# Grouped attention and a spectral filter on one core: queries kept in DRAM, longer batches, and the filter's last part turned

## The chip, the core and the metric

The kernel runs on one core of a Trainium2 chip. Times are microseconds of the device (us) for one execution. The core has five engines that this document speaks of: PE (matrix multiplications, with PEld as its loads of stationary operands), ACT (ScalarE, here above all `exp`), DVE (VectorE), POOL (GpSimd) and SP, which here only issues DMAs. Matrix products are written to PSUM, eight banks of 128 x 512 float32; everything else is in SBUF or in DRAM.

## The reference

The two halves of the output have nothing to do with each other. The first is attention of 16 query heads over one common head of keys and values, the second a filter in the frequency domain:

```python
B, S, D, H = 1, 2048, 448, 16; Dh = 28
# first half
q = (A_x @ wq) per head;  k = A_x @ wk;  v = A_x @ wv
p = softmax(q @ k.T * Dh**-0.5);  a = concat_heads(p @ v) @ wo
# second half
X = rfft2(B_x) * (w_r + 1j*w_i);  b = irfft2(X)      # 2048 x 448
out = concatenate([a, b], axis=-1)
```

All inputs and outputs are float32.

## The kernel before

**Stages.** The first 70 us project the queries, keys and values and run the first part of the filter. From there on the program is one long weave: attention, in which PE, ACT and DVE hand tiles to each other, with pieces of the filter and of the output projection pushed in between. A short tail finishes the last 512 rows of the first output.

**Attention.** The 2048 queries are 4 chunks `c` of 512; the 16 heads are 4 groups `g` of 4; the 2048 keys are 16 blocks `kc` of 128. A *step* is one (c, g, kc): four score matmuls, one per head, each 128 keys x 512 queries into a PSUM bank (line 872); four tiles of `exp` on ACT (line 816) into two buffers of 2 x 512 columns; and the products with the values (line 827), four heads side by side in 32 columns of the array, summed over the 16 `kc` in one PSUM bank `po`. In the trace a float32 product shows as two instructions, so the value products of a step are 8 rows of line 827. There are 256 steps. Scores and value matrices use different precisions: operands of type float32r (`qa`, `ka`) run in one pass; where float32 exactness is wanted the kernel splits an operand in a high part and a rest and adds three such products (`mm3`).

**Batches.** Steps are handled in batches. A batch first issues all its score matmuls and then, in `flush`, the value products of its steps (without its last one, but with the last one of the batch before, `kept`). So PE goes from scores to value products and back once per batch. The scores of the last step of a batch come early among the others (token `k`): DVE copies them from PSUM into the buffers `k` (line 878), and ACT makes their `exp` in place as two instructions of 128 x 1024 (line 895) while PE is busy with the value products. That keeps ACT fed while no new scores come.

**The table of order.** PE, ACT and DVE run in the order in which the Python code records their instructions. `PLAN` has one string per batch, made by `spread(n, units, ...)`: `-` is a score matmul whose `exp` ACT makes from PSUM, `k` one that DVE copies away, `e` one of the last step that ACT reads from PSUM itself. Letters are *units*: `A` and `B` are the second part of the filter (`fft2_a`, `fft2_b`), `W` is one of four pieces of an output projection of 128 rows (`wo_unit`), `Z` a piece of the filter's third part. In front of all this, `take()` hands out the PSUM bank that by the planner's clocks comes free first, `put()` queues DVE work that may be done later, and `passed()` and `at_once()` move the clocks and record queued work when its time has come.

**The third part of the filter** works on 8 slices `q`. `fft3_a` (line 660, twice per slice, e = 0 and 1) makes the spectrum over rows in float32, and DVE copies it to `z` (line 663). `fft3_b` (line 674, twice per slice, v = 0 and 1) multiplies with the cosines and sines `cs3`: the spectrum is the stationary operand, the constants are the 113 moving columns, in float32; its result has rows of the image on the 128 partitions. DVE makes a sum and a difference from PSUM (lines 678 to 680), POOL two further sums (lines 684 and 685), and SP writes 128 x 452 to `ob`.

**Queries.** `qraw` holds all projected queries in SBUF (128 x 4 x 2048). For each group `build_q` takes one chunk of it, shifts it, splits it on DVE into `qh` and `ql`, and SP places these by nine DMAs in `qa`, of which there are two. After its chunk's four groups are built, a chunk of `qraw` is read only in a branch for very large scores, which the inputs do not take.

**Tail.** The last group's values are divided and transposed on DVE; `partial` adds up three of four groups for each of four blocks of rows, `final` adds the fourth with float32 operands (line 918); ACT copies the block from PSUM (line 741) and issues its DMA.

Of the kernel before, what the change touches and what calls it, by code (L numbers as in the profile page):

```python
# [37 lines left out]
def spread(n, units, lazy=4, start=0.9, rest=0.85):  # L38

    m = 4 * n - 4  # L40
    out = [(float(i), "-") for i in range(m)]
    out += [(j + 0.5 if j < lazy else m + 0.1 * j, "k" if j < lazy else "e") for j in range(4)]
# [4 lines left out]
PLAN = ["eeee"] + ["eeeeF"] + [spread(2, "", 0, 1.05)] + 3 * [spread(2, "", 0)] + [spread(5, "A", 4, 1.6)]  # L47
PLAN += [spread(5, "BA", 4, 0.9, 0.6)] + [spread(5, "A")] + 6 * [spread(5, "BA", 4, 0.9, 0.6)]
PLAN += [spread(5, "BA", 4, 0.75, 0.6)] + 3 * [spread(5, "BA", 4, 0.9, 0.6)] + 2 * [spread(6, "X")]
PLAN += [spread(5, "BA", 4, 0.9, 0.6)] + [spread(6, "BAX")] + [spread(5, "BAB", 4, 0.9, 0.6)]  # L50
PLAN += [spread(6, "BX")] + [spread(6, "Y")] + [spread(5, "")] + 2 * [spread(6, "Y")]
PLAN += [spread(6, "Y", 4, 0.9, 0.6)] + [spread(6, "X")] + [spread(6, "X", 4, 0.9, 0.6)] + [spread(6, "X")]
PLAN += [spread(6, "Y")] + [spread(6, "X", 4, 0.9, 0.6)] + 3 * [spread(6, "Y")]
PLAN += [spread(6, "Y", 4, 0.9, 0.73)] + [spread(6, "Y")] + [spread(6, "Y", 4, 0.9, 0.73)]
PLAN += 3 * [spread(6, "X")] + [spread(6, "Y")] + [spread(6, "X", 4, 0.9, 0.73)] + [spread(5, "Y")]
PLAN += [spread(6, "Y")] + [spread(6, "Y", 4, 1.2)] + [spread(5, "Y")]
# [6 lines left out]
def kernel(ctx: ExitStack, tc: tile.TileContext, t: dict):  # L63
# [17 lines left out]
    bits = cp.tile([1, 1], F32, name="bits")  # L81
    t1 = dp.tile([128, 32, DF], F32, name="t1")
# [428 lines left out]
    pp = pools.enter_context(tc.tile_pool(name="pp", bufs=P_BUFS))  # L511
# [125 lines left out]
    def fft3_consts():  # L637
        fc["cs3"] = fp.tile([113, 4, 113], F32, name="cs3", tag="cs", bufs=1)
        behind(nc.gpsimd.dma_start(fc["cs3"], t["cs3"]), begun[-1])
# [15 lines left out]
    def fft3_a(q, e):  # L655
# [6 lines left out]
        z = c2["z", q, e] = fp.tile([113, 2, 4, 64], F32, name=f"z{e}", tag=("wi", "cst")[e])  # L662
        nc.vector.tensor_copy(z[:w], pz[:w].rearrange("p j (r n) -> p r j n", r=2))
        at_once()
        give(bank)

    def fft3_b(q, v):
        ze, zo = c2["z", q, 0], c2["z", q, 1]
        cs3 = fc["cs3"]
        js = slice(2 * v, 2 * v + 2)  # L670
        bank = take()
        py = bank[:, :452].rearrange("p (k n) -> p k n", k=4)
        for k, (z, w, r) in enumerate(((ze, 113, 0), (zo, 112, 0), (zo, 112, 1), (ze, 113, 1))):
            mm(py[:, k], z[:w, r, js], cs3[:w, k], start=True, stop=True)  # L674
        passed(888)
        y1 = fp.tile([128, 2, 2, 113], F32, name="y1", tag="pwr")
        m = fp.tile([128, 2, 113], F32, name="m", tag="us", bufs=1)
        nc.vector.tensor_copy(m, py[:, 2:4])
        nc.vector.tensor_tensor(y1[:, :, 0], py[:, 0:2], m, op=ALU.add)
        nc.vector.tensor_tensor(y1[:, :, 1], py[:, 0:2], m, op=ALU.subtract)  # L680
        at_once(1100)
        give(bank)
        yo = fp.tile([128, 4, 113], F32, name="yo", tag="pwi")
        nc.gpsimd.tensor_tensor(yo[:, 0:2], y1[:, 0], y1[:, 1], op=ALU.add)  # L684
        nc.gpsimd.tensor_tensor(yo[:, 2:4], y1[:, 0], y1[:, 1], op=ALU.subtract)
# [242 lines left out]
    for k in (0, 1):  # L928
        partial(k)
# [197 lines left out]
```

## Time and profile before

| | before |
|---|---|
| median of 3 runs | 642.26 us (642.26 to 642.81) |
| the profiled execution | 642.82 us, its span 641.0 us |
| PE busy | 635.7 us, 99% |
| ACT busy | 550.7 us, 86% |
| DVE busy | 372.3 us, 58% |
| POOL busy | 80.1 us, 12% |
| granted TensorE clock | 1.00 |

PE is busy nearly all the time by this count, but the count has the overlap of successive matmuls and any short wait inside a row in it. Where PE loses time has to be read from the starts of its instructions in the timeline: the distance from one start to the next, against what the same kind of instruction takes elsewhere.

### The profile page before, as it was taken

What the parts mean: (1) busy time and instruction counts of PE and PEld (TensorE: products, weight loads), DVE (VectorE), ACT (ScalarE), POOL (GpSimd) and SP (SyncE); (2) the same over time, 40 slices, a digit from 0 to 9 for tenths busy, and PEclk for the clock granted to TensorE, in tenths of its full rate; (3) what the DMA queues carried; (4) which work ended last, traced back from release to release, by engine and by line L of the source; (5) the groups of instructions that cost most, each with busy time, mean ns of one, the idle gap of its engine ahead of it and who ended that gap; (6) DMA issues with size and microseconds to landing.
All of it is one profiled execution on the core that took longest, in us unless ns stands there. A gap on an engine that the chain in (4) does not pass through costs nothing.

```text
span 641.0 us, 12024 instructions
## 1 busy us (share of the span) xinstructions
PE 635.7 (99%) x4470; PEld 381.8 (60%) x4470; DVE 372.3 (58%) x683; ACT 550.7 (86%) x1011; POOL 80.1 (12%) x150
## 2 busy tenths in 40 slices
PE   9999999999999999999999999999999999999997
PEld 6877655556555556655655566556655566556555
DVE  5999628889997934766543523264545332264521
ACT  5554999999999998988899898998999898998981
POOL 3021401011311110000120300003031100200110
PEclk9999999999999999999999999999999999999999
DMA  8755971554835521214241403123241303140001
GB/s 271 268 161 159 262 175 47 143 126 111 205 102 128 142 59 49 79 47 136 63 103 44 115 16 85 39 57 92 55 120 43 88 15 81 44 127 2 30 31 60
DMA packets 36113, 63.83 MB, mean 100 GB/s; under 512 B 7905, under 2 KB 23922, under 8 KB 35084
## 3 DMA queue, kind: packets, MB, share of 16 engines
q1 hardware_dynamic: 30832, 49.60, 28.0%
q0 software_dynamic: 4640, 12.48, 7.8%
q10 hardware_dynamic: 576, 0.92, 0.4%
q8 instruction: 36, 0.59, 0.4%
q14 instruction: 29, 0.24, 0.1%
HBM read 30.04 MB, written 14.75 MB: 70 GB/s over the span
## 4 chain that ended last, share of the span: by engine, by line
PE 98%; DMA 1%; ACT 0%; SPq 0%; issue 0%; ACTq 0%
PE s L872 31%; PE s L827 22%; PE sx L827 9%; PE s L347 6%; PE po L872 5%; PE po L827 4%; PE s L736 4%; PE sx L872 4%; PE s L145 2%; PE s L674 2%; PE s L660 2%; PE pbb L164 1%; DMA raw<-wq 1%; PE s L562 1%; PE s L561 1%; PE s L563 1%
## 5 line engine op out<-in xcount | busy, mean ns | idle before, releaser
L816 ACT ACTIVATE p<-s 128x512 f32<-128x512 f32 x650 | 345.9, 631 | 33.4 <-PE s L872 27.5
L872 PE MATMUL s<-qa,ka 128*128 128x512 f32 x798 | 236.1, 405 | 0.0
L872 PEld LDWEIGHTS s<-qa,ka 128*128 128x128 f32 x798 | 146.7, 188 | 67.7 <-issue 26.8
L878 DVE COPY k<-s 128x512 f32<-128x512 f32 x129 | 82.5, 682 | 106.6 <-PE s L872 106.6
L827 PE MATMUL s<-p,vs 128*32 128x512 f32 x1024 | 121.7, 595 | 0.0
L895 ACT ACTIVATE k<-k 128x1024 f32<-128x1024 f32 x88 | 90.3, 1108 | 0.0
L827 PEld LDWEIGHTS s<-p,vs 128*32 128x32 f32 x1024 | 30.8, 109 | 67.6 <-issue 65.6
L816 ACT ACTIVATE p<-po 128x512 f32<-128x512 f32 x89 | 56.2, 631 | 9.2 <-PE po L872 8.5
L816 ACT ACTIVATE p<-sx 128x512 f32<-128x512 f32 x85 | 53.6, 630 | 3.1 <-PE sx L872 1.9
L827 PE MATMUL sx<-p,vs 128*32 128x512 f32 x416 | 49.3, 594 | 0.0
L872 PE MATMUL po<-qa,ka 128*128 128x512 f32 x120 | 49.2, 410 | 0.0
L872 PE MATMUL sx<-qa,ka 128*128 128x512 f32 x106 | 42.4, 400 | 0.0
L700 POOL DMA_DIRECT2D ol<-ol x36 | 18.1, 510 | 135.9 <-DVE ol L723 69.0
L827 PE MATMUL s<-k,vs 128*32 128x512 f32 x256 | 33.4, 594 | 0.0
L684 POOL TENSOR_TENSOR yo<-y 128x226 f32<-128x226 f32 x16 | 9.5, 596 | 188.0 <-DVE y L680 110.9
L872 PEld LDWEIGHTS po<-qa,ka 128*128 128x128 f32 x120 | 22.5, 188 | 14.6 <-issue 9.2
L827 PEld LDWEIGHTS sx<-p,vs 128*32 128x32 f32 x416 | 12.5, 110 | 27.9 <-issue 27.6
L831 DVE STREAM_TRANSPOSE osb<-s 128x512 f32<-128x512 f32 x10 | 7.2, 715 | 37.0 <-PE s L827 37.0
L878 DVE COPY k<-po 128x512 f32<-128x512 f32 x29 | 19.8, 681 | 14.3 <-PE po L872 14.3
L827 PE MATMUL po<-p,vs 128*32 128x512 f32 x208 | 25.0, 595 | 0.0
L872 PEld LDWEIGHTS sx<-qa,ka 128*128 128x128 f32 x106 | 19.9, 188 | 6.7 <-issue 2.5
L347 PE MATMUL s<-xh,wqh 128*128 128x512 f32 x56 | 23.0, 410 | 0.1
(217 smaller groups left out, 788.1 us busy)
## 6 DMA issues: line engine op xcount, KB each, us to landing
qa<-qa SPq DMA_DIRECT2D x15, 512.0 KB
raw<-xa SPq DMA_DIRECT2D x16, 256.0 KB
xb<-xb SPq DMA_DIRECT2D x8, 512.0 KB
qa<-qh SPq DMA_DIRECT2D x64, 64.0 KB
qa<-ql SPq DMA_DIRECT2D x60, 64.0 KB
ob<-yo SPq DMA_DIRECT2D x16, 226.0 KB
t<-bs SPq DMA_DIRECT2D x16, 225.0 KB
wr<-wr POOLq DMA_DIRECT2D x16, 225.0 KB, 4.2
```

The lines of the kernel that those rows point to most:

```text
L145: mm(pa[r0:r0 + 32, e, o0:o0 + n], f[:, 2 * r + k, 2 * p + e, h], cs1[:, 2 * r + k, :n], start=True, stop=True)
L347: mm(pq, w[:, j, gs], x[:, j], start=(j == 0 and n == 0), stop=(j == 3 and n == 1))
L660: mm(pz[:w, j], c2["c", q][:, j, o0:o0 + w], c2["F", q][:, j], start=True, stop=True)
L674: mm(py[:, k], z[:w, r, js], cs3[:w, k], start=True, stop=True)
L684: nc.gpsimd.tensor_tensor(yo[:, 0:2], y1[:, 0], y1[:, 1], op=ALU.add)
L700: nc.gpsimd.dma_start(ol[c][o, g].bitcast(F32), ol[c][r, 0].bitcast(F32))
L736: mm(p, x[c][:, g, s], w, start=(g == 0 and n == 0), stop=(g == NG - 1 and n == 2))
L816: nc.scalar.activation(tiles[-1][:, h % 2], sc, AF.Exp, scale=SCALE)
L827: mm(po[c, g][32 * i:32 * i + 32], vs[:, kc], ps[i // 2][:, i % 2], start=(n == 1), stop=(n == 16))
L872: begun.append(mm(sc, ka[:, kc * 128:(kc + 1) * 128], qa[c, g][:, h], start=True, stop=True))
L878: nc.vector.tensor_copy(keep[h // 2][:, h % 2], sc)
L895: nc.scalar.activation(p, p, AF.Exp, scale=SCALE)
```

## The change

The edit has five parts.

1. **Queries in DRAM.** When the last group of a chunk has been built, SP copies the chunk of `qraw` to a new DRAM tile `qd` (three times, 1 MB each), and its place in SBUF becomes two more buffers for `exp` tiles. The eight buffers `p` are now named tiles that pass through a queue `spans`. Only the branch for large scores reads `qd` back.
2. **Longer batches.** `PLAN` is written anew. From step 102 on a batch has 6, 7 or 8 steps; there are 46 batches instead of 50 (2 of one step, 4 of two, 1 of four, 14 of five, 5 of six, 18 of seven, 2 of eight; before 2, 4, 0, 18, 26, 0, 0). In 24 batches with more than four `k` or `e`, the last *two* steps are put aside: the second-last one in two buffers of `spans`, with its value products at the end of the same flush, the last one in `k` as before. Copies `k` are spread over more of the batch.
3. **The filter's third part.** `fft3_a` splits its result in a high part and a rest on DVE. `fft3_b` is turned: the constants, split once, are the stationary operand, and the spectrum is 256 moving columns, in three float32r products for each of two terms. The result has 113 columns of the image on the partitions. The last sum and difference are now made on DVE, once per slice, instead of on POOL, and go out as 112 partitions and one single row (`oc`).
4. **Tail.** `final` uses three float32r products instead of a float32 one, for which DVE splits the last values; the DMAs of the first three blocks are issued by SP, and the last block is copied half by ACT and half by DVE.
5. **Order.** `build_q` for the next group is recorded two steps earlier.

```diff
-def spread(n, units, lazy=4, start=0.9, rest=0.85):
+def spread(n, units, lazy=4, start=0.9, rest=0.85, apart=1.0):
+    late = 8 if lazy > 4 else 4
+    m = 4 * n - late
...
-PLAN += [spread(6, "Y")] + [spread(6, "Y", 4, 1.2)] + [spread(5, "Y")]
+PLAN += [spread(7, "ZZ", 8, 0.9, 0.6, 2.0)] + [spread(7, "ZZ", 8, 0.6, 0.85, 2.0)]
...
-    pp = pools.enter_context(tc.tile_pool(name="pp", bufs=P_BUFS))
+    pp = pools.enter_context(tc.tile_pool(name="pp", bufs=1))
+    spans = deque(pp.tile([128, 2, CW], F32, name=f"p{i}") for i in range(P_BUFS))
...
-        z = c2["z", q, e] = fp.tile([113, 2, 4, 64], F32, name=f"z{e}", tag=("wi", "cst")[e])
-        nc.vector.tensor_copy(z[:w], pz[:w].rearrange("p j (r n) -> p r j n", r=2))
-        at_once()
+        ...
+        z = pz[:w].rearrange("p j (r n) -> p r j n", r=2)
+        nc.vector.tensor_copy(h[:w], z)
+        nc.vector.tensor_tensor(l[:w], z, h[:w].bitcast(F32), op=ALU.subtract)
+        at_once(1330)
...
-        for k, (z, w, r) in enumerate(((ze, 113, 0), (zo, 112, 0), (zo, 112, 1), (ze, 113, 1))):
-            mm(py[:, k], z[:w, r, js], cs3[:w, k], start=True, stop=True)
+        py = bank[:113].rearrange("p (k n) -> p k n", k=2)
+        for i, k in enumerate((v, v + 2)):
+            ...
+            a, b = fc["cs3h"][:w, k], fc["cs3l"][:w, k]
+            mm(py[:, i], a, h, start=True, stop=False)
+            mm(py[:, i], b, h, start=False, stop=False)
+            mm(py[:, i], a, l, start=False, stop=True)
...
-        nc.gpsimd.tensor_tensor(yo[:, 0:2], y1[:, 0], y1[:, 1], op=ALU.add)
-        nc.gpsimd.tensor_tensor(yo[:, 2:4], y1[:, 0], y1[:, 1], op=ALU.subtract)
-        r0 = (2 * q + v) * 128
-        nc.sync.dma_start(t["ob"][r0:r0 + 128], yo)
+        if v:
+            x0, d = c2["y", 0], fp.tile([113, 2, 256], F32, name="yo", tag="pwi")
+            def total():
+                nc.vector.tensor_tensor(x, x0, x, op=ALU.add)
+                nc.sync.dma_start(t["ob"][q, 0], x[:112])
+                nc.sync.dma_start(t["oc"][q:q + 1], x[112:113])
+            def difference():
+                nc.vector.tensor_tensor(d, x0, x, op=ALU.subtract)
+                nc.sync.dma_start(t["ob"][q, 1], d[:112])
+            put(("y", q), [(600, difference), (600, total)], True)
...
+        c, g = divmod(step, 64)
+        if c < NC - 1 and g == 40:
+            need(("q", 4 * c + 3))
+            behind(nc.sync.dma_start(qd[:, :, c * CW:(c + 1) * CW], qraw[:, :, c * CW:(c + 1) * CW]), begun[-1])
+        if c < NC - 1 and g == 43:
+            spans.extend(qraw[:, i:i + 2, c * CW:(c + 1) * CW] for i in (0, 2))
-        if step % 16 == 3 and step < 240:
+        if step % 16 == 1 and step < 240:
...
+        stay = 1 + (sum(k in "ke" for k in tokens) > 4)
+        keep = [[pp.tile([128, 2, CW], F32, name="k", bufs=4) for _ in range(2)]]
+        if stay > 1:
+            keep.append([spans.popleft() for _ in range(2)])
...
-        flush(steps[:1] + kept if n > 4 else kept + steps[:-1], steps[1:-1] if n > 4 else [])
-        kept = steps[-1:]
+        flush(normal[:1] + kept if n > 4 else kept + normal, normal[1:] if n > 4 else [])
+        kept = [(*s, ps, False) for s, ps in zip(steps[:-stay - 1:-1], keep)]
+        for i in reversed(range(stay)):
+            ...                                   # exp of keep[i]
+            if i:
+                flush([kept.pop()])
+                spans.extend(keep[i])
...
     def final(k):
-        p = ws[k]
-        mm(p, on[:, 128 * k:128 * k + 128], w3, start=False, stop=True)
-        wo_out(p, c, k, True)
+        p, s = ws[k], slice(128 * k, 128 * k + 128)
+        h, l = oh[c][:, NG - 1, s], ol[c][:, NG - 1, s]
+        mm(p, h, woh[:, NG - 1], start=False, stop=False)
+        mm(p, l, wox[:, NG - 2], start=False, stop=False)
+        mm(p, h, wol[:, NG - 1], start=False, stop=True)
+        wo_out(p, c, k, k + 1)
```

What this does to the order of instructions is seen at three places. The first is `fft3_b` on PE, the first of it, in the kernel before (names carry the tile's number behind the last underscore; `s0` to `s5`, `sx` and `po` are PSUM banks; line 872 are scores, line 674 is `fft3_b`, `z0` and `z1` the spectrum for e = 0 and 1):

```order
L872 MATMUL po_1105<-qa_3142,ka_67 128x512
L674 MATMUL s3_87<-cs3_1346,z0_3392 128x113
L674 MATMUL s3_87<-cs3_1346,z1_3398 128x113 x2
L674 MATMUL s3_87<-cs3_1346,z0_3392 128x113
L674 MATMUL s4_88<-cs3_1346,z0_3392 128x113
L674 MATMUL s4_88<-cs3_1346,z1_3398 128x113 x2
L674 MATMUL s4_88<-cs3_1346,z0_3392 128x113
L872 MATMUL s2_86<-qa_3142,ka_67 128x512
```

And the first `fft3_b` of the changed kernel on PE (line 917 are scores now, lines 699 to 701 the three products; `zh` and the reused tile `c2` are the high parts, `zl` the rests):

```order
L917 MATMUL sx_1113<-qa_2972,ka_67 128x512
L699 MATMUL s2_87<-zh_3228,cs3h_3122 113x256
L700 MATMUL s2_87<-zh_3228,cs3l_3123 113x256
L701 MATMUL s2_87<-zl_3229,cs3h_3122 113x256
L699 MATMUL s2_87<-c2_3124,cs3h_3122 113x256
L700 MATMUL s2_87<-c2_3124,cs3l_3123 113x256
L701 MATMUL s2_87<-zl_3258,cs3h_3122 113x256
L917 MATMUL s1_86<-qa_2972,ka_67 128x512
```

Four products of 113 columns have become six of 256 columns, and the second unit, which followed at once (bank `s4`), now stands apart among the scores.

The second place is the end of a flush on PE, in a batch of six steps before (line 827 are the value products, summed in the bank `po_1105`; a row stands for two heads of a step):

```order
L827 MATMUL po_1105<-k_3105,vs_68 32x512 x2
L827 MATMUL po_1105<-k_3106,vs_68 32x512 x2
L827 MATMUL po_1105<-p_3236,vs_68 32x512 x2
L827 MATMUL po_1105<-p_3246,vs_68 32x512 x2
L827 MATMUL po_1105<-p_3251,vs_68 32x512 x2
L827 MATMUL po_1105<-p_3256,vs_68 32x512 x2
L827 MATMUL po_1105<-p_3268,vs_68 32x512 x2
L827 MATMUL po_1105<-p_3287,vs_68 32x512 x2
L827 MATMUL po_1105<-p_3305,vs_68 32x512 x2
L827 MATMUL po_1105<-p_3308,vs_68 32x512 x2
L872 MATMUL s4_88<-qa_2830,ka_67 128x512
```

And the end of a flush of a batch of seven in the changed kernel on PE (line 863 are the value products; `p0` to `p7` are the named buffers, `qraw` the buffers in the place of the queries, four heads of a step in one row):

```order
L863 MATMUL s4_89<-k_3205,vs_68 32x512 x2
L863 MATMUL s4_89<-p6_1057,vs_68 32x512 x2
L863 MATMUL s4_89<-p7_1058,vs_68 32x512 x2
L863 MATMUL s4_89<-p4_1055,vs_68 32x512 x2
L863 MATMUL s4_89<-p5_1056,vs_68 32x512 x2
L863 MATMUL s4_89<-qraw_66,vs_68 32x512 x4
L863 MATMUL s4_89<-p0_1051,vs_68 32x512 x2
L863 MATMUL s4_89<-p1_1052,vs_68 32x512 x2
L863 MATMUL s4_89<-p2_1053,vs_68 32x512 x2
L863 MATMUL s4_89<-p3_1054,vs_68 32x512 x2
L917 MATMUL s2_87<-qa_2972,ka_67 128x512
```

The flush has seven steps instead of six between two turns to scores, and its last two rows read the two buffers (`p2`, `p3`) of the second-last step, which was put aside.

The third place is ACT around a flush before, where the two instructions of the last step (line 895) stand between the `exp` tiles (line 816) of two batches:

```order
L816 ACTIVATE p_3423<-s4_88 128x512
L816 ACTIVATE p_3423<-sx_1104 128x512
L816 ACTIVATE p_3426<-s5_89 128x512
L816 ACTIVATE p_3426<-s3_87 128x512
L895 ACTIVATE k_3353<-k_3353 128x1024
L895 ACTIVATE k_3354<-k_3354 128x1024
L816 ACTIVATE p_3459<-s1_85 128x512
L816 ACTIVATE p_3459<-s4_88 128x512
L816 ACTIVATE p_3469<-s5_89 128x512
L816 ACTIVATE p_3469<-po_1105 128x512
```

And ACT around a flush of a batch of seven in the changed kernel (line 852 for tiles from PSUM, lines 928 to 946 for the steps put aside: `p2` and `p3` the second-last, `k` the last):

```order
L852 ACTIVATE p1_1052<-s0_85 128x512
L852 ACTIVATE p1_1052<-s1_86 128x512
L928 ACTIVATE p3_1054<-sx_1113 128x512
L928 ACTIVATE p3_1054<-s5_90 128x512
L946 ACTIVATE p2_1053<-p2_1053 128x512 x2
L942 ACTIVATE k_3333<-k_3333 128x1024
L942 ACTIVATE k_3334<-k_3334 128x1024
L852 ACTIVATE p6_1057<-s2_87 128x512
L852 ACTIVATE p6_1057<-s3_88 128x512
L852 ACTIVATE p7_1058<-s0_85 128x512
L852 ACTIVATE p7_1058<-sx_1113 128x512
L852 ACTIVATE p4_1055<-s2_87 128x512
```

ACT now has two steps put aside between the tiles of two batches instead of one, and the first of them (`p3` from PSUM, `p2` in place) feeds the end of the flush that is already running.

More of the change, by code (lines that the diff above doesn't have):

```diff
@@ L33 @@
 P_BUFS = 8
-def spread(n, units, lazy=4, start=0.9, rest=0.85):
-    m = 4 * n - 4
+def spread(n, units, lazy=4, start=0.9, rest=0.85, apart=1.0):
+    late = 8 if lazy > 4 else 4
+    m = 4 * n - late
     out = [(float(i), "-") for i in range(m)]
-    out += [(j + 0.5 if j < lazy else m + 0.1 * j, "k" if j < lazy else "e") for j in range(4)]
+    out += [(apart * j + 0.5 if j < lazy else m + 0.1 * j, "k" if j < lazy else "e") for j in range(late)]
     out += [(m * (j + start) / (len(units) + rest) - 0.4, u) for j, u in enumerate(units)]
@@ L805 @@
     kept, po = [], {}
[L807 removed]
+    waiting, count = deque(), {}
     def exps():
[L811 removed]
+        while waiting and (waiting[0][2] % 2 or spans):
             sc, tiles, h = waiting.popleft()
             if h % 2 == 0:
[L814 to L815 removed]
+                tiles.append(spans.popleft())
             nc.scalar.activation(tiles[-1][:, h % 2], sc, AF.Exp, scale=SCALE)
@@ L836, in flush @@
             if normal:
-                held[0] -= 2
+                spans.extend(ps)
                 exps()
@@ L858 @@
         new, lazy, x = [], [], {"-": 0, "k": 0}
-        keep = [pp.tile([128, 2, CW], F32, name="k", bufs=4) for _ in range(2)]
+        stay = 1 + (sum(k in "ke" for k in tokens) > 4)
+        keep = [[pp.tile([128, 2, CW], F32, name="k", bufs=4) for _ in range(2)]]
+        if stay > 1:
+            keep.append([spans.popleft() for _ in range(2)])
         for k in tokens:
```

139 lines of the change are left out of this document (81 added, 58 removed).

## The prediction

> **What bounds the kernel now.** I read the page first: who is busy, and which engine carries the chain that ended last.
>
> ```profile
> span 641.0 us, 12024 instructions
> PE 635.7 (99%) x4470; PEld 381.8 (60%) x4470; DVE 372.3 (58%) x683; ACT 550.7 (86%) x1011; POOL 80.1 (12%) x150
> PE 98%; DMA 1%; ACT 0%; SPq 0%; issue 0%; ACTq 0%
> ```
>
> PE is on 98% of the chain. So an edit is worth what it takes off PE's row of work, or off the waits in that row. The other engines matter where they make PE wait. The timeline of PE shows one batch of six steps, from flush to flush:
>
> ```profile
> 335.12 1.06 PE L827 MATMUL s<-p,vs 128*32 128x512 f32 x8
> ...
> 340.40 0.50 PE L872 MATMUL sx<-qa,ka 128*128 128x512 f32 x1
> ...
> 340.98 1.33 PE L872 MATMUL s<-qa,ka 128*128 128x512 f32 x5
> 342.14 0.40 PE L872 MATMUL sx<-qa,ka 128*128 128x512 f32 x1
> ...
> 343.77 1.04 PE L660 MATMUL po<-fi,c 128*113 128x128 f32 x8
> ...
> 345.44 1.17 PE L872 MATMUL s<-qa,ka 128*128 128x512 f32 x4
> ```
>
> Durations overlap, so I go by starts. A score takes 0.233 us (340.98 to 342.14 for five). A value product takes 0.1075 us: the next view, the chain in order of time, has runs of 40 in 4.43 and of 48 in 5.29, so 0.86 per step and 0.13 that each run adds. The first two scores after a flush take 0.58 (340.40 to 340.98), 0.11 more than two others. The last score before a flush takes 0.34, again 0.11 more (106.41 to 106.75, second fence below). So a turn to the value products and back costs 0.13 + 0.11 + 0.11 = 0.35 us per batch.
>
> ```profile
> 70.52 2.16 PE s L872 x8
> 96.31 4.43 PE s L827 x40
> 230.81 2.22 PE s L736 x11
> 335.19 5.29 PE s L827 x48
> 626.45 3.85 PE s L736 x18
> ```
>
> ```profile
> 105.10 0.37 PE L561 MATMUL s<-bh,g1h 128*128 128x450 f32 x1
> ...
> 105.71 0.40 PE L872 MATMUL sx<-qa,ka 128*128 128x512 f32 x1
> ...
> 106.41 0.42 PE L872 MATMUL s<-qa,ka 128*128 128x512 f32 x1
> 106.75 1.06 PE L827 MATMUL s<-p,vs 128*32 128x512 f32 x8
> ...
> 356.88 1.04 PE L674 MATMUL po<-cs,z 113*128 113x113 f32 x8
> ...
> 358.59 1.40 PE L872 MATMUL s<-qa,ka 128*128 128x512 f32 x5
> ```
>
> Here are the units: two `fft3_b` in 1.71 us (356.88 to 358.59), 0.855 each, and three float32r products of 450 columns in 0.61 (105.10 to 105.71), 0.203 each. Two `fft3_a` take 1.67 (343.77 to 345.44), and the eleven products of four `W` 2.22.
>
> With these, a batch has a floor: steps x (4 x 0.233 + 0.86) + 0.35 + its units. Stages between two flushes' ends show how far the real ones lie above it (first column the stage in us, then its length, PE, PEld, DVE and ACT busy):
>
> ```profile
> 142.74:153.26 10.52, 10.52 (x70) 6.00 (x66) 9.78 (x19) 9.83 (x18) 0.53 (x1) 1.00 0.34 100
> 317.45:327.47 10.02, 10.02 (x64) 4.64 (x61) 5.84 (x11) 9.42 (x18) 2.54 (x5) 1.00 0.25 59
> 458.62:471.78 13.16, 13.16 (x93) 7.49 (x89) 8.02 (x16) 11.98 (x22) 5.08 (x9) 1.00 0.47 117
> 471.78:484.62 12.84, 12.84 (x92) 7.60 (x88) 3.86 (x6) 11.89 (x22) 0.00 (x0) 1.00 0.22 63
> 563.93:577.24 13.31, 13.31 (x88) 7.92 (x84) 9.30 (x18) 12.00 (x22) 0.00 (x0) 1.00 0.43 114
> ```
>
> The first, five steps with an `A` and a `B`, has a floor of 10.53: no stall, although DVE is 93% busy. The second has no unit: floor 9.31, stall 0.7; ACT is what it waits for, with 9.4 us of work. The third (two `fft3_b`, and DVE with query and output work as well) stalls 0.3, the fourth 0.05, the fifth (one `W` block) 0. Over all 256 steps the floor is 239 (1024 scores) + 220 (2048 value rows) + 20 (`A`, `B`) + 27 (`W`) + 27 (`Z`) + 17.5 (50 turns) = 550.5, and the stretch from the first score to the tail is 626.45 - 70.52 = 555.9, with a piece of the filter's first part in it (`F`), which I put at 1 us. So all stalls together are about 4.5 us. That is the most that a better order alone can bring.
>
> **The change part by part.** *Longer batches.* 46 turns instead of 50: 4 x 0.35 = -1.4 us. Nothing covers a turn, so this is certain up to its price (-1.0 to -1.7).
>
> *The turned `fft3_b`.* No row has a float32r product of 256 columns. By proportion to 450 columns it takes 0.203 x 256/450 = 0.115, six of them 0.69; by the slope between 450 and 512 columns (0.030 for 62) it is 0.109, six 0.65. From above: 0.233/2 = 0.117 by proportion to the scores, 0.70. If the loads of weights did not hide, a step would also pay the load of a score, 0.188 us:
>
> ```profile
> L872 PEld LDWEIGHTS s<-qa,ka 128*128 128x128 f32 x798 | 146.7, 188 | 67.7 <-issue 26.8
> ```
>
> But scores run every 0.233 with such a load each, so it lies beside the matmul ahead of it. I take 0.70, against 0.855: 16 x -0.155 = -2.5 us (-3.3 with 0.65; +14.6 with the loads in the open). [...]
>
> *What the turned form and the longer batches put on DVE.* The share of DVE in 40 slices of the span, and rows by shape:
>
> ```profile
> DVE  5999628889997934766543523264545332264521
> ...
> L878 DVE COPY k<-s 128x512 f32<-128x512 f32 x129 | 82.5, 682 | 106.6 <-PE s L872 106.6
> L663 DVE COPY z<-s 113x512 f32<-113x512 f32 x5 | 3.5, 691 | 5.7 <-PE s L660 5.7
> L678 DVE COPY m<-s 128x226 f32<-128x226 f32 x11 | 4.3, 393 | 7.4 <-PE s L674 7.0
> ```
>
> The subtraction in `fft3_a` is 16 x 0.69, the sums taken over from POOL 16 x 0.69 by the same row, the three operations of `fft3_b` 48 x 0.05 more in proportion to their columns, 67 more copies `k` (243 instead of 176) at 0.68: 11.0 + 11.0 + 2.4 + 45.6 = 70 us. This lies beside PE: DVE has 372 of 641 us busy, and nearly all of the new work comes after step 100, in the last 21 slices, where the digits are mostly 2 to 6. A batch of seven with eight `k` and two `fft3_b` has 8 x 0.68 + 2 x 1.3 + 1.4 = 9.4 us of its own, and some 2 us of query and output work, against 14.3 us of PE: a share of 0.8, below the 0.93 of the first stage above, which has no stall. I cost it at nothing; if PSUM banks come free late, it costs what the third stage shows, 0.3 us per batch.
>
> *ACT.* A tile of 512 takes 0.5 us (nine from 343.40 to 347.88), 1024 of them 512 us against 546 of PE. A batch of seven needs 14.0 against 12.9 and its units, 0.8 to 2.4: enough in all but one (step 172, one `Z`), which I cost like the stage without a unit at half its stall, 0.4. The row that asks for care is the step put aside for the same flush:
>
> ```profile
> 338.20 2.02 ACT L895 ACTIVATE k<-k 128x1024 f32<-128x1024 f32 x2
> 341.00 0.60 ACT L816 ACTIVATE p<-sx 128x512 f32<-128x512 f32 x1 [0.77 <-PE sx L872]
> ...
> 343.40 4.61 ACT L816 ACTIVATE p<-s 128x512 f32<-128x512 f32 x9
> 347.88 0.63 ACT L816 ACTIVATE p<-po 128x512 f32<-128x512 f32 x1
> ```
>
> The flush starts at 335.12; ACT is through with the tiles from PSUM 3.1 us later and with the step put aside 5.1 us later, and then idles 0.77. In a batch of seven that step is wanted as the seventh, 6 x 0.86 + 0.05 = 5.2 us after the start: just in time, and ACT then has the last step to work on where it idles now. I cost it at nothing (0 to +0.3 in each of the 24 batches).
>
> *Stalls.* 4.5 us now; two or three places with too few units remain (steps 8, 35, 172), the rest is a trade of the idle 0.77 of ACT against a fuller DVE. I leave the sum at 4.5: change 0 (-3 to +7).
>
> *Tail.* `final` and the next `partial` follow each other every 2.58 us:
>
> ```profile
> 630.13 0.91 PE L918 MATMUL s<-w,osb 128*128 128x448 f32 x2
> 632.71 0.91 PE L918 MATMUL s<-w,osb 128*128 128x448 f32 x2
> L927 DVE STREAM_TRANSPOSE osb<-osb 128x128 f32<-128x128 f32 x4 | 1.2, 312 | 0.1
> 637.19 0.54 ACT L741 ACTIVATE yb<-s 128x448 f32<-128x448 f32 x1 [0.41 <-PEq L940]
> ```
>
> Nine products of 0.203 leave 0.75 for the float32 `final`; three float32r ones take 0.61: 4 x -0.14 = -0.6. The last copy, 0.54, is halved between two engines: -0.2 (nearest row, 128 columns: 0.31). DVE's eight small operations more, 2.5 us at that row's 0.31, hide behind the two `partial` (626.45 to 630.13, 3.7 us) ahead of the first `final`. Sum -0.8 (-1.2 to 0).
>
> *Queries in DRAM, earlier `build_q`.* 3 MB more.
>
> ```profile
> DMA packets 36113, 63.83 MB, mean 100 GB/s; under 512 B 7905, under 2 KB 23922, under 8 KB 35084
> ```
>
> The first copy of a chunk stands on SP between the pieces of `qa` of the next group and their doubling, so that this waits for 1 MB more: 10 us at the mean rate of the span, and the queue is not full there. The group is wanted two batches after its `build_q`, some 20 us: hidden. If half of the 10 us were uncovered once, +5.
>
> Sum: -1.4 - 2.5 + 0 - 0.8 = -4.7 against the profiled execution, 642.82 us: 638.1. The median of the runs lies 0.56 below that one: **637.6 us**.
>
> **The rivals.** *The stalls go too* (0.22). With ACT fed through the flush, most of the waits of PE's weight loads on ACT would vanish:
>
> ```profile
> PEld s L872 <- ACT p L816: 10.6, 45, 0.3
> ```
>
> 45 waits of 0.24 us, of which part is hidden. If 3 of the 4.5 us go: 634.6; with `fft3_b` at 0.65, 633.8, and with a turn at 0.42, 633.5. Against it: DVE is fuller and the batches without units stay.
>
> *DVE hands banks back late* (0.16). 13 batches carry `Z` and eight or so `k`; a split of 1.4 us stands ahead of a copy `k`, and the score that wants this bank waits, with all scores behind it. At the price of the third stage, 0.3, it is 13 x 0.3 = 3.9: 641.5, no change (0.09). At twice that and more, 0.7, it is 9.1: 646.7, slower (0.07). It decides from 0.36 us per batch. For it: the third stage; against it: the first and fifth.
>
> *The flush ends on a wait* (0.05). If ACT enters a flush 0.3 us later than at 335.12, PE waits 0.3 in each of 24 flushes: +7.2, 644.8, slower. It decides from 0.2 us per flush. Against it: with eight scores of 28 read by DVE, ACT is less behind when the flush begins.
>
> *Turning does not pay* (0.02). If a load waited for the matmul ahead, a product would cost 0.188 + 0.115: 16 x (1.82 - 0.855) instead of -2.5 gives 655.5. [...]
>
> **How the numbers follow.** Forecast 0.55, stalls gone 0.22, DVE 0.09 and 0.07, flush 0.05, loads 0.02. The range goes from 633.5 (stalls gone and the cheaper matmul) to 643.0 (DVE's cheaper case and its bounds). A measurement of this kernel tells 0.2%, 1.3 us, from no change. Faster is the forecast, the stalls gone and a small part of DVE's cheaper case: 0.79; same 0.07; slower 0.14.
>
> **What would show it.** PE: the group of `fft3_b` products at six starts 0.115 apart, 0.70 a unit; scores at 0.233 and value products at 0.86 a step unchanged; a run of 56 value rows in 6.15 us without a gap ahead of its last eight. ACT: no idle after the flush, where it has 0.77. DVE: near 440 us busy, and the last copies `k` before a flush not late. POOL: no sums. The tail 0.8 us shorter. I am wrong if PE's starts show gaps ahead of scores that wait for DVE, gaps ahead of the last eight value products, or products of 256 columns at 0.2 us or more.

## The result, and the profile after

The changed kernel takes 640.64 us (median of 11 runs, 640.13 to 642.72) where the kernel before, run beside it, takes 642.59 (642.02 to 642.81): a ratio of 0.9975, 95% interval 0.9967 to 0.9984. It is faster by 1.95 us, inside the range and of the forecast sign, but far less than the 4.7 forecast. Its profiled execution took 640.64 us, with a span of 638.9.

The page of the changed kernel, to set beside the lines shown of before:

```profile
span 638.9 us, 12167 instructions
PE 628.8 (98%) x4442; PEld 378.3 (59%) x4442; DVE 440.8 (69%) x793; ACT 547.0 (86%) x983; POOL 61.1 (10%) x118
DVE  5999648889998934856766845386687446476652
PE 96%; DMA 1%; SPq 1%; DVE 0%; issue 0%; ACT 0%; ACTq 0%; DVEq 0%
```

DVE is busy for 440.8 us, as worked out (372 + 70), and POOL's sums are gone. New in the chain that ended last is a percent of SP's sequencer (SPq). Two views show that PE's work shrank as forecast: a turned unit in PE's timeline, and the chain in order of time around a flush of seven steps:

```profile
319.53 0.29 PE L699 MATMUL s<-zh,cs3h 113*113 113x256 f32 x1
319.66 0.28 PE L700 MATMUL s<-zh,cs3l 113*113 113x256 f32 x1
...
320.13 0.29 PE L701 MATMUL s<-zl,cs3h 112*113 112x256 f32 x1
320.25 0.62 PE L917 MATMUL s<-qa,ka 128*128 128x512 f32 x2
```

```profile
296.74 6.14 PE s L863 x56
```

Six products of 256 columns take 0.72 us from start to start (319.53 to 320.25), and 56 value rows 6.14 without a gap ahead of the last eight.

**The weave** is the stretch from the first score to the first product of the tail. Here are its rows before and after (stage, length, busy time of PE, PEld, DVE, ACT and POOL, granted clock, share and GB/s of the DMAs):

```profile
70.45:626.38 555.93, 555.89 (x3574) 319.85 (x3573) 308.24 (x550) 508.54 (x936) 61.87 (x114) 1.00 0.33 85
```

```profile
70.14:621.79 551.65, 549.77 (x3543) 315.48 (x3541) 374.40 (x651) 504.99 (x908) 42.65 (x83) 1.00 0.35 92
```

It is 4.3 us shorter, about the forecast (3.9). But in the second row PE's count falls 1.9 us short of the length, where before it fills it to 0.04. That is one place, seen in PE's timeline and, for the same time, in SP's:

```profile
504.94 0.37 PE L771 MATMUL s<-wol,oh 128*128 128x448 f32 x1
507.16 0.45 PE L771 MATMUL s<-woh,oh 128*128 128x448 f32 x1 [1.84 <-DMA oh<-ol]
```

```profile
498.70 0.85 SPq L228 DMA_DIRECT2D qa<-ql  x1
499.64 1.92 SPq L732 DMA_DIRECT2D oh<-ol  x3
501.74 0.52 SPq L230 DMA_DIRECT2D qa<-qa  x1
502.30 0.59 SPq L732 DMA_DIRECT2D oh<-ol  x1
```

A `W` unit needs the four small moves `oh<-ol` (8 KB each) of group (c=2, g=3). Three go out from 499.64 on; the fourth stands behind the doubling of the next group's queries (`qa<-qa`, 512 KB), is issued at 502.30, and PE can go on only at 507.16, 2.0 us late.

**The tail**, measured from DVE's transpose of the last group's values to the end of the span, went from 14.5 us (626.50 to 641.0) to 17.0 (621.91 to 638.9). The timeline of the changed kernel's tail, with one line of the waits of SP:

```profile
621.91 0.72 DVE L867 STREAM_TRANSPOSE osb<-s 128x512 f32<-128x512 f32 x1 [5.77 <-PE s L863]
...
631.24 0.55 ACT L779 ACTIVATE yb<-s 128x448 f32<-128x448 f32 x1 [1.87 <-PE s L970]
632.34 0.36 ACT L779 ACTIVATE yb<-po 128x224 f32<-128x224 f32 x1 [0.56 <-DMA oa<-yb]
...
632.73 0.39 DVE L781 COPY yb<-po 128x224 f32<-128x224 f32 x1 [4.96 <-ACT yb L779]
```

```profile
SPq L995 <- SPq L995: 2.6, 1, 2.6
```

Before, the same two views read:

```profile
626.50 0.72 DVE L831 STREAM_TRANSPOSE osb<-sx 128x512 f32<-128x512 f32 x1 [5.64 <-PE sx L827]
```

```profile
SPq L940 <- SPq L940: 10.2, 2, 7.3
```

Three things are new. The last block waits for a buffer that a DMA still reads (0.56). Its second half, on DVE, starts only when ACT's half is done; both write one tile, which is the likely reason, but no run gave the halves two tiles. And SP waits 2.6 us in its own sequencer at line 995. There every engine loads a guard word and branches around the code for large scores: SP's load runs from 633.54 to 634.03, its branch ends at 634.15, and its next instruction comes at 636.76. In the kernel before SP was there early, with its waits beside the tail (10.2 us in two waits). Now SP has the output DMAs ahead of it. From the last copy's end to the span's end it was 3.3 us before (637.73 to 641.0) and is 5.8 after (633.12 to 638.9).

### The profile page after: what moved, and what is told of

The parts are those of the page before. It is cut to its first block, busy times and chain, and to the rows that moved or that the text cites. A ratio compares the mean times of both kernels' runs of the same rounds, so it can differ in the third digit from the quotient of the medians.

```text
span 638.9 us, 12167 instructions
## 1 busy us (share of the span) xinstructions
PE 628.8 (98%) x4442; PEld 378.3 (59%) x4442; DVE 440.8 (69%) x793; ACT 547.0 (86%) x983; POOL 61.1 (10%) x118
## 4 chain that ended last, share of the span: by engine, by line
PE 96%; DMA 1%; SPq 1%; DVE 0%; issue 0%; ACT 0%; ACTq 0%; DVEq 0%
PE s L863 30%; PE s L917 28%; PE s L357 6%; PE sx L917 5%; PE po L917 5%; PE po L863 4%; PE s L771 4%; PE s L155 2%; PE sx L771 1%; PE s L675 1%; PE pbb L174 1%; PE s L572 1%; PE s L573 1%; PE s L574 1%; PE sx L675 1%; PE s L305 1%
## 5 line engine op out<-in xcount | busy, mean ns | idle before, releaser
L852 ACT ACTIVATE p<-s 128x512 f32<-128x512 f32 x410 | 223.7, 637 | 28.7 <-PE s L917 28.0
L917 PE MATMUL s<-qa,ka 128*128 128x512 f32 x751 | 226.6, 403 | 0.0
L917 PEld LDWEIGHTS s<-qa,ka 128*128 128x128 f32 x751 | 137.2, 188 | 62.1 <-issue 27.7
L852 ACT ACTIVATE qraw<-s 128x512 f32<-128x512 f32 x138 | 79.2, 654 | 5.0 <-PE s L917 4.9
L917 PE MATMUL sx<-qa,ka 128*128 128x512 f32 x143 | 57.4, 401 | 0.0
L863 PE MATMUL s<-qraw,vs 128*32 128x512 f32 x432 | 55.4, 593 | 0.0
L852 ACT ACTIVATE p<-sx 128x512 f32<-128x512 f32 x60 | 38.6, 644 | 3.9 <-PE sx L917 3.8
L863 PEld LDWEIGHTS s<-qraw,vs 128*32 128x32 f32 x432 | 13.5, 110 | 30.8 <-issue 29.0
L923 DVE COPY k<-sx 128x512 f32<-128x512 f32 x27 | 18.5, 684 | 13.0 <-PE sx L917 13.0
L923 DVE COPY k<-po 128x512 f32<-128x512 f32 x17 | 11.6, 685 | 21.5 <-PE po L917 21.4
L852 ACT ACTIVATE qraw<-sx 128x512 f32<-128x512 f32 x34 | 21.8, 640 | 2.6 <-PE sx L917 2.6
```

The source lines that it names most:

```text
L852: nc.scalar.activation(tiles[-1][:, h % 2], sc, AF.Exp, scale=SCALE)
L863: mm(po[c, g][32 * i:32 * i + 32], vs[:, kc], ps[i // 2][:, i % 2], start=(n == 1), stop=(n == 16))
L917: begun.append(mm(sc, ka[:, kc * 128:(kc + 1) * 128], qa[c, g][:, h], start=True, stop=True))
L923: nc.vector.tensor_copy(keep[i][h // 2][:, h % 2], sc)
```

## The experiments

Times are medians of each run's executions. The kernel before ran beside each of the four groups of runs, with medians of 642.70, 642.79, 642.62 and 642.58.

### Who issues the last DMAs

All four output DMAs on ACT's queue, the split kept:

```diff
-            (nc.scalar if last == 4 and not e else nc.sync).dma_start(t["oa"][r0:r0 + 128, s], y[:, s])
+            (nc.scalar if last else nc.sync).dma_start(t["oa"][r0:r0 + 128, s], y[:, s])
```

> The kernel after, with the four output DMAs of the last column block issued by ACT's queue instead of SP's (the last block stays copied in two halves); all else unchanged. Theory A (the output DMAs on SP put SP's load of the guard word and its branch, 2.6 us, and the program's end behind the last of them): the tail becomes 2 to 3 us shorter, 637.6 to 638.6. Rival A2 (the tail is long because the halves of rows land late or because the last copy waits for a buffer): nothing changes, 640.3 to 641.0. Rival A3 (the queue is at fault only for the order on it, not for the branch): 0.5 to 1 us less, 639.6 to 640.1.

The same, and the last block copied whole by ACT:

```diff
-        for e in ((0, 1) if last == 4 else (0,)):
-            s = slice(e * D // 2, (e + 1) * D // 2) if last == 4 else slice(0, D)
+        for e in (0,):
+            s = slice(0, D)
```

> The kernel after, with the four output DMAs of the last column block on ACT's queue and the last block copied whole by ACT, as the kernel before does it; turned third part and longer batches stay. Theory A: 0.2 to 0.6 us above the run with the split kept, 638.0 to 639.0. Rival A2 (the split and its half rows are what costs): 0.5 to 2 us below that run.

And the other way round, in the kernel before:

```diff
-        (nc.scalar if on_act else nc.sync).dma_start(t["oa"][r0:r0 + 128], y)
+        nc.sync.dma_start(t["oa"][r0:r0 + 128], y)
```

> The kernel before, with the four output DMAs of its last column block issued by SP instead of ACT; nothing else. Theory A: slower by 2 to 3 us, 644.6 to 645.6, with the branch of SP behind the last output DMA. Rival A2: unchanged, 642.3 to 642.9.

Measured: 640.49, 638.05 and 644.98 us. The third is as expected: moving four DMAs to SP cost the kernel before 2.3 us. Its tail and the wait of SP:

```profile
626.16 0.72 DVE L831 STREAM_TRANSPOSE osb<-sx 128x512 f32<-128x512 f32 x1 [5.64 <-PE sx L827]
...
636.68 0.54 ACT L741 ACTIVATE yb<-s 128x448 f32<-128x448 f32 x1 [0.21 <-PEq L940]
```

```profile
SPq L940 <- SPq L940: 2.5, 1, 2.5
```

The copies end as early as before, but the end comes 5.6 us behind the last copy (637.22 to 642.8) instead of 3.3, with 2.5 us in SP's sequencer. The first run missed its expectation: its median lies where the rival had it, as if nothing had changed. Its trace shows two reasons. Its tail is 15.5 us (623.78 to 639.3), only 1.5 shorter, because another engine took SP's place: DVE, which makes the last half copy, is now the last to come to the guard, and SP waits for it at the end:

```profile
SPq L1181 <- DVEq L995: 1.5, 1, 1.5
```

With the copy whole on ACT the tail is 14.4 (624.04 to 638.4), against the expectation, which held the split to be worth 0.2 to 0.6: in these two traces it costs 1.1. The other reason lies at 505 us: in both traces the tail begins later than in the changed kernel (623.78 and 624.04 for 621.91). In the first the wait there is as long as in the changed kernel (2.18 us from start to start for 2.22), but the granted clock is 0.56 over 3.5 us behind it; in the second the wait is longer too (3.03 us), and the clock is 0.50 for some 3.5 us behind it as well. The next experiments and the last section come back to this. The second kernel's five executions fall in two groups, 638.01 to 638.05 at a mean clock of 0.999 to 1.0 and 639.98 and 640.22 at 0.997; the trace is of the slowest of them.

The guard itself was then left out, in both kernels: the load of the word and the branch with all its body.

```diff
-    rv = nc.values_load(bits.bitcast(I32)[0:1, 0:1])
-    with tc.If(rv > int(np.float32(BOUND).view(np.int32))), tc.tile_pool(name="g1", bufs=1) as g1:
-        ...
```

> The kernel after without the guard at the end (the load of the guard word and the branch on every engine, with the branch's body, are left out). Theory A: SP has nothing to do behind its last output DMA, 2 to 2.6 us less, 638.0 to 638.6. Rival: DMAs that SP issues land or are counted later than ACT's whatever follows, 640.2 to 640.8.

> The kernel before without the guard at the end (the same part left out). Theory A: SP's load and branch stand beside the tail already, 0 to 0.6 us less, 642.0 to 642.6. Rival (the guard delays the end by itself, wherever the DMAs are issued): 640.0 to 640.6.

Measured: 637.17 and 642.09 us. Without it the changed kernel gains 3.5, the kernel before 0.7. The tail of the changed kernel is then 13.5 us (621.86 to 635.4), with the output DMAs still on SP. So it is not the landing of SP's DMAs that costs, but that the guard's load and branch stand behind them. The gain is more than the expected 2 to 2.6. The traces give its two parts: from the last copy's end to the span's end it is 2.8 us instead of 5.8, since load, branch and wait took SP 3.2 us together (633.54 to 636.76); and the last block found its buffer free and was copied 0.56 earlier (at 631.78). The DMA that frees this buffer was issued at the same time in both, so this second part may be chance.

### The wait at 505 us

The four small moves of that one group on POOL:

```diff
-            nc.sync.dma_start(oh[c][o, g].bitcast(F32), ol[c][r, 0].bitcast(F32))
+            (nc.gpsimd if (c, g) == (2, 3) else nc.sync).dma_start(oh[c][o, g].bitcast(F32), ol[c][r, 0].bitcast(F32))
```

> The kernel after, with the four small moves oh<-ol of one group (column block 2, group 3) issued by POOL instead of SP, so that none of them stands behind the 512 KB doubling of the queries on SP. Theory B (the 1.8 to 2.2 us for which PE waits at about 505 us is that place in SP's queue): 638.4 to 639.0, and no wait on oh<-ol in that batch. Rival B2 (the norm itself is late, since its step is flushed at the end of a longer batch; the moves land late by any queue): 640.3 to 640.8, the wait stays above 1 us.

Measured: 638.72 us, 1.9 below the changed kernel. PE passes the place without a wait:

```profile
504.72 0.36 PE L771 MATMUL s<-wox,ol 128*128 128x448 f32 x1
504.92 0.36 PE L771 MATMUL s<-wol,oh 128*128 128x448 f32 x1
505.12 0.39 PE L917 MATMUL s<-qa,ka 128*128 128x512 f32 x1
```

The rival fell: DVE's part ends at 496.9, 6 us before the unit starts, and moves of 8 KB on POOL's queue landed 2.3 us after their issue (`ol<-ol`, median in the changed kernel at this place), so the values are in time by a free queue. The opposite edit put all four moves behind the doubling:

```diff
+            if (c, g) == (2, 3):
+                behind(mv, begun[-1])          # and spares() called at the first W unit of g == 3
```

> The kernel after with all four small moves of group (2, 3) behind the 512 KB doubling on SP instead of the last one alone. Theory B: PE's wait at 505 us grows from 2.2 to 2.8 to 3.5 us. If an idle PE of that length brings the granted clock to half for some 3.5 us, as in the two traces with tails on ACT (idle 2.16 and 3.01 us, clock 0.50 for 3.5 us behind it, about 1.7 us more), in every execution: 642.4 to 643.8. If that drop was chance: 641.2 to 642.0. If the place in the queue is not the cause: 640.3 to 640.9.

Measured: 642.64 us (640.98 to 645.06), 2.0 above the changed kernel. PE's timeline, and the granted clock behind the wait (stage, length, PE busy, clock, DMA):

```profile
504.62 0.37 PE L773 MATMUL s<-wol,oh 128*128 128x448 f32 x1
507.41 0.45 PE L773 MATMUL s<-woh,oh 128*128 128x448 f32 x1 [2.42 <-DMA oh<-ol]
...
508.46 0.63 PE L921 MATMUL s<-qa,ka 128*128 128x512 f32 x1
508.89 0.63 PE L921 MATMUL sx<-qa,ka 128*128 128x512 f32 x1
```

```profile
508.00:511.50 3.50, 3.50 (x10) 0.55 0.18 66
```

The wait grew by only 0.6 us (2.79 from start to start instead of 2.22), but behind it scores start every 0.43 us instead of 0.233, since the granted clock is 0.55 over the next 3.5 us: 10 matmuls in this stretch where the changed kernel, at full clock, has 17.

```profile
508.00:511.50 3.50, 3.50 (x17) 1.00 0.18 66
```

Seven matmuls at 0.23 are 1.6 us. With 0.6 for the wait that is 2.2; measured are 2.0 between the medians and 1.7 between the two traced executions.

### Mended, and the old order

Three mends in one: the small moves of group (2, 3) on POOL, the tail's DMAs and its whole last copy on ACT, and a buffer for each of the four blocks.

```diff
-        y = pp.tile([128, D], F32, name="yb", tag=f"p{k % 2}") if last else ap.tile([128, D], F32, name="ya")
+        y = pp.tile([128, D], F32, name="yb", tag=f"p{k}") if last else ap.tile([128, D], F32, name="ya")
```

> The kernel after with three mends together: the four small moves of group (2, 3) on POOL, the last column block's output DMAs on ACT's queue with the last block copied whole by ACT, and a buffer of its own for each of the four output blocks. From the runs so far: 638.7 with the moves on POOL, less 2.6 for the tail (from the last flush's transpose to the end 17.0 us in the kernel after, 14.4 with ACT's queue and one copy), less 0.5 to 0.9 for the wait on a buffer (0.56 and 0.90 in those two traces): 635.2 to 635.7. If the parts overlap (the last DMA's landing decides, not the copy): 636.0 to 636.5. The time in every execution within 0.5 of the others, since no long wait of PE is left.

Measured: 635.60 us (635.19 to 636.02), as expected: a ratio of 0.9891 to the kernel before (0.9875 to 0.9907), and the fastest kernel of this study. Its tail runs from 619.74 to 633.4, 13.7 us, and its weave is:

```profile
69.93:619.61 549.68, 549.64 (x3542) 315.56 (x3541) 374.46 (x651) 504.93 (x908) 44.95 (x88) 1.00 0.36 92
```

Then the mended kernel with the old `PLAN`, all else kept:

```diff
-PLAN = ["eeee"] + ["eeeeF"] + [spread(2, "", 0, 1.05)] + 2 * [spread(2, "", 0)] + [spread(5, "A", 4, 1.6)]
...
+PLAN = ["eeee"] + ["eeeeF"] + [spread(2, "", 0, 1.05)] + 3 * [spread(2, "", 0)] + [spread(5, "A", 4, 1.6)]
...
```

> The mended kernel (three mends together) with the order of batches of the kernel before: 50 batches of 2, 5 and 6 steps, one step put aside in each; the turned third part, the copies in DRAM and the tail as in the mended kernel. If the longer batches are worth their turns alone (4 x 0.35): 1.2 to 1.7 above the mended kernel. If they also take waits away (the floor of the batches fits both weaves and leaves 6.3 us of waits before and 4.2 after, without the one at 505 us): 3.2 to 3.8 above it. If DVE's added copies eat the turns: the same as it or faster.

Measured: 642.62 us, 7.0 above the mended kernel: nearly twice what the larger of the expectations had. Its weave:

```profile
70.19:627.00 556.81, 556.77 (x3543) 315.03 (x3541) 331.23 (x584) 504.99 (x936) 44.47 (x86) 1.00 0.34 91
```

That is 0.9 us longer than in the kernel before, with the same batches and with units that take 16 x 0.135 = 2.2 us less of PE. So in the old order no gain from the turned third part is seen; the queries in DRAM, the earlier `build_q` and DVE's sums are in this kernel too, and this difference does not tell them apart. A fourth product in each sum (low part by low part) shows from the other side what PE's time is worth there; first in the mended kernel, then in its version with the old order:

```diff
-            mm(py[:, i], a, l, start=False, stop=True)
+            mm(py[:, i], a, l, start=False, stop=False)
+            mm(py[:, i], b, l, start=False, stop=True)
```

> The mended kernel with a fourth product in each sum of the turned third part (low part by low part): two more matmuls of 256 columns in each of 16 units, 32 x 0.12 = 3.8 us of PE. Theory C (in the long batches PE ends the batch): 3.0 to 3.9 above the mended kernel, 638.6 to 639.5. Rival: hidden behind ACT or DVE there as well, 0 to 1.5 above it.

> The same fourth product in the mended kernel with the old order of short batches. Theory C (ACT ends the batches that hold a third part, 0.35 to 0.6 us after PE could): only 0 to 1.5 of the 3.8 us show, 642.6 to 644.1. Rival C2 or C3 (PE's row waits for banks, the added products come on top): 3 to 3.9 above, 645.6 to 646.5.

Measured: 638.85 us, 3.25 above the mended kernel, and 644.04, 1.4 above the old order. Of the same 3.8 us of PE, 85% show with the long batches and 37% with the short ones. Most of PE's added time counts in the former; something else ends most of the latter's batches with `Z`.

What that is took three runs: the old order with eight scores put aside instead of four (from step 109 on, in the batches of six with `W` too), with the two `Z` of a batch apart instead of adjacent (the first about three scores earlier, the second five later), and with both. The edit of a batch with `Z` in each:

```diff
-spread(6, "Y")
+spread(6, "Y", 8, 0.9, 0.6, 1.75)       # eight put aside
+spread(6, "ZZ", 4, 0.9, 0.6)            # apart
+spread(6, "ZZ", 8, 0.9, 0.6, 1.75)      # both
```

> The mended kernel with the short batches (as in the run with the old order), but from step 109 on each batch of six puts eight scores aside instead of four, so that ACT has a second step put aside to work on during the flush; nothing is longer. Theory C (the turned third part gains nothing in short batches since ACT, not PE, ends a batch: 20 tiles of 0.49, 2.1 for the step put aside and 1.1 to 1.3 us in which it waits for the first score after the flush, 13.0 us in all; a second step put aside fills that wait): most of the 7 us between the two orders comes back, 636.5 to 638.5, and batches with two Z last 12.6 to 12.8 instead of 13.0 to 13.3. Rival C2 (DVE's added work for the third part holds PSUM banks back; eight copies make that worse): 642.6 or above. Rival C3 (it is the length or where the units stand): 641 to 642.6.

> The mended kernel with the old order of short batches, but with the two Z units of a batch set apart (some eight scores between them) instead of one behind the other. Theory D (each turned Z unit holds its PSUM bank about 0.7 us longer behind DVE's subtraction, and two in a row leave the scores behind them without banks; apart, each is made good before the next): batches with two Z go from 13.05 to 13.3 us down to 12.6 to 12.9, 16 of them by 0.3 to 0.5: 4.8 to 8 us less than with the units adjacent, 635.5 to 638. Theory C (ACT ends these batches, wherever the units stand): 641.5 to 643, as with the units adjacent.

> The same with the two Z units set apart and eight scores put aside in each batch of six from step 109 on. Theory D: as much below the run with eight put aside and adjacent units (640.8) as the other pair differs, 636 or less; with the gain of 1.8 from the eight put aside, close to or below the mended kernel with its long batches less their turns, 635.0 to 637.0. Theory C: 640.5 to 641.2. If DVE is too full with both: above 642.

Measured: 640.79, 645.99 and 638.70 us. Setting the units apart costs 3.4 with four put aside and gains 2.1 with eight; neither theory alone has that, and none of the three times lies in a range that was expected for it. Two successive batches of six steps show why, the first with two `fft3_b`, the second with two `fft3_a`; ahead of them the floors by PE's own times, 12.52 and 12.75. The old order of the mended kernel, then units apart, then both:

```profile
327.16:340.19 13.03, 13.03 (x89) 7.12 (x85) 6.23 (x12) 12.28 (x23) 0.00 (x0) 1.00 0.26 73
340.19:353.29 13.10, 13.10 (x92) 7.49 (x89) 9.07 (x15) 11.80 (x22) 0.00 (x0) 1.00 0.09 21
```

```profile
327.36:340.69 13.33, 13.33 (x88) 7.23 (x84) 6.23 (x12) 12.17 (x23) 0.00 (x0) 1.00 0.25 72
340.69:354.03 13.34, 13.34 (x92) 7.53 (x89) 9.16 (x15) 11.78 (x22) 0.00 (x0) 1.00 0.10 22
```

```profile
326.73:339.38 12.65, 12.65 (x89) 7.22 (x85) 8.54 (x16) 12.17 (x21) 0.00 (x0) 1.00 0.45 114
339.38:352.55 13.17, 13.17 (x93) 7.47 (x89) 11.64 (x19) 11.93 (x20) 0.00 (x0) 1.00 0.07 17
```

With units apart and four put aside, a batch lasts 13.33 whichever unit it holds. It is read here as a cycle of ACT, from its timeline in that kernel:

```profile
327.96 1.09 ACT L842 ACTIVATE p<-s 128x512 f32<-128x512 f32 x2 [0.21 <-PE s L907]
...
337.53 2.21 ACT L932 ACTIVATE k<-k 128x1024 f32<-128x1024 f32 x2
...
341.29 1.09 ACT L842 ACTIVATE p<-s 128x512 f32<-128x512 f32 x2 [1.56 <-PE s L907]
```

Twenty tiles take 9.6 us (327.96 to 337.53), the step put aside 2.2, and then ACT waits 1.6 us for the first score behind the flush: 13.3. Where a second step put aside stands in that wait, the batch with `fft3_b` is PE's: 12.65, 0.13 above its floor. The batch with `fft3_a` stays 0.4 above. DVE is busy 11.6 of its 13.2 us there, and its added subtraction (0.69 us) holds the unit's bank longer; that this is what remains was not tested by itself. Both together (638.70) leave 3.1 us to the mended kernel, of which four turns are 1.4; the rest was not taken apart.

## Why the prediction was right and where it failed

The sum had the right sign and most of its costs of work, and failed on waits that it did not have: in the tail (-0.8 forecast, +2.5 measured) and at 505 us (2.0). About 2.3 us of other waits, which it had left standing, went and made up for part of that.

*The turned `fft3_b`.* Right: 0.72 us a unit for 0.70, six starts 0.12 apart, with loads of 0.17 to 0.18 us (lines 699 to 701) beside the matmuls, so -2.2 us of PE for -2.5. The rival in which loads lie open is out. But the term was counted as time, and in the old order no gain of it is seen; how much of it counts in the long batches was measured only by adding work (85%), not by turning it back.

*Longer batches and stalls.* The terms were -1.4 and 0. The weave became 4.3 shorter for a forecast of 3.9, by two errors that nearly cancel. Without the wait at 505 us it is 6.2 shorter (555.93 to 549.68 in the mended kernel): the terms have 3.9 of this, so some 2.3 us of the other waits went, as the rival "the stalls go too" had it. That was no merit of the sum, and the rival's mechanism is not borne out either. The waits of PE's weight loads that the profile puts down to ACT, summed over the weave, were 61 of 15.2 us before and are 90 of 22.9 us in the mended kernel; and ACT still idles behind a flush, where the prediction gave "no idle" as a sign, for instance in the changed kernel:

```profile
303.40 1.09 ACT L852 ACTIVATE p<-s 128x512 f32<-128x512 f32 x2 [1.12 <-PE s L917]
318.17 0.60 ACT L852 ACTIVATE qraw<-sx 128x512 f32<-128x512 f32 x1 [1.01 <-PE sx L917]
```

What took the waits away was not isolated. The other error is the one wait of 2.0 us. The forecast checked small moves only as part of a general "stalls" term; it did not walk the moves of the shifted `norm` past SP's queue, where a 512 KB doubling had come to stand ahead of one of them.

*DVE at nothing.* Right in its load, and right in the long batches (85% of added PE work shows). Whether it was free in the short ones is open: the batch with `fft3_a` that stays 0.4 above its floor was not taken apart.

*ACT.* The idle of 0.77 us ahead of the next scores was seen, but given no price. It was the thing to price: in the short batches it is, by the reading above, ACT's wait in a cycle that ends the batch as soon as PE's part gets shorter.

*Tail.* This is the step that failed most: -0.8 forecast, +2.5 measured. The products were shorter as said, and in the mended kernel the tail is 0.8 shorter than before (13.7 to 14.5), in part by luck: about half of that lies behind the last copy (2.9 us for 3.3), where the prediction had nothing. But the move of the DMAs from ACT to SP was costed at nothing, without looking at what SP still has to do behind them: the guard's load and branch, 2.1 to 2.3 us in the kernel before with that one move. The halves were taken to run side by side, at -0.2; they run one behind the other, on a buffer that was not free.

*Queries in DRAM* showed no wait of PE in the trace: its count falls short of the weave at the one place only. The flush did not end on a wait either (6.14 us for 56 rows).

The sum from the changed to the mended kernel is 5.0 us: 1.9 for the small moves (638.72), 3.1 for the tail (17.0 to 13.7 in the traces). The mended kernel is at 635.6, 2.0 below the forecast, which fits the 2.3 us of waits that went in the weave.

## What to carry to other kernels

When a DMA is moved to another engine, read that engine's program to its last instruction: what stood beside the work may now stand behind it, and here, at the end of the kernel, nothing hid it (5.8 us behind the last copy instead of 3.3). Before work is taken off the engine that is 99% busy, look for the next engine's cycle through the same stage (its tiles, its own work in the gap, its wait), because a shorter bound pays only where that cycle is shorter too; here the turned product showed no gain in the old order, and 3.9 us of the 7.0 between the two orders came back by putting a second step aside for ACT and setting the units apart. And price each small transfer by what stands ahead of it in its queue: 8 KB behind 512 KB cost PE 2 us once, which was as much as the whole measured gain.

## What the hardware showed that was not expected

Behind a short idle of PE the clock fell in some traces and not in others. After 2.79 us between two starts the granted clock was 0.55 over the next 3.5 us, in which PE ran seven matmuls fewer, 1.6 us of scores; with 2.22 us, in the changed kernel, it stayed at 1.00; with 2.18 us, in the kernel with the tail on ACT, it was 0.56 over the same stretch:

```profile
508.00:511.50 3.50, 3.50 (x10) 0.56 0.18 66
```

So the length of the idle alone did not decide: in the 3 us ahead of that stretch (505.0 to 508.0) PE was idle for 2.4, 1.84 and 1.82 us. What did was not shown, and no run tested it. In the kernel with the tail on ACT the clock was 0.96 over the next 3.5 us and 1.00 from 515 on.

The other is the price of this program's end: loading one guard word took SP 0.5 us, and behind the branch around unused code it stood still for another 2.5 to 2.6 (line 995 in the changed kernel, line 940 with the DMAs moved to SP). This went unseen as long as SP came there early; left out, the guard gained 3.5 us in the changed kernel and 0.7 in the one before.
